# Query features turned by VectorE and through DRAM instead of by TensorE, and gated tiles stored in longer pieces

## The chip, the cores and the metric

The kernel runs on one core of a Trainium2 chip. The metric is the device time of one execution in microseconds (us); the time of a kernel is the median of its runs. The engines are named as in the profile: PE is TensorE's matrix multiply, PEld its weight load, DVE is VectorE, ACT ScalarE, POOL GpSimd, SP SyncE, which issues most of the DMAs. DMAs issued by GpSimd wait in GpSimd's own instruction queue, those of SP in SP's.

## What is computed

A layer over 2048 tokens of width 512, all in float32: the input plus a linear attention with 32 heads and learned softmax features, plus a gated MLP whose gate mixes tokens. Cut to what matters:

```python
def reference(A_x, A_wqkv, A_w_phi, A_wo, B_x, B_w_in, B_w_sp, B_b_sp, B_w_out):
    xn = _layernorm(A_x)
    # A: q, k, v per head of width 16; features = [softmax(p), softmax(-p)], p = q @ w_phi[h]
    #    kv = phi_k^T v, z = sum of phi_k over the tokens
    #    o = (phi_q kv) / (phi_q z + 1e-6);   A = o @ wo
    # B: z = gelu(xn @ w_in); z1, z2 = halves of width 688; z2 = layernorm(z2)
    #    u = z1 * (w_sp @ z2 + b_sp);         B = u @ w_out
    return A_x + A + B
```

## The kernel before

The tokens are 16 tiles of 128. A float32 operand of a large product is split into a rounded part `h` and a rest `l`, and `mm3` makes each product from three matmuls (hence lines 56, 57 and 58).

First part (to about 220 us): the projections of each tile; the query features before their normalisation go to DRAM (`e_d`), and so do the inner halves `z1` (`z1_d`). Second part (to about 290 us): the other halves `z2` and their split. Third part (to about 488 us): the product of `w_sp` with `z2`, pair of tiles by pair of tiles, in seven sub-products per block (`products`, 32 steps `n`), whose left operands are loaded by SP (`wf`) and made by ScalarE and VectorE (`prep_a`) two steps ahead. Behind every fourth step `drain` adds the sub-products up and `gate` multiplies with gelu of `z1`. The gated tiles `u` have the tokens in their partitions and are needed with the features there, for the last product. `turn` does this in two steps: VectorE transposes all 32x32 blocks of the pair (L796), and four DMAs, one for each 32 partitions, store the blocks to `u_d` so that they come to stand in their transposed places (L799). Since a partition then holds runs of only 32 floats that belong together, the pieces have 128 bytes. Pair 6 is stored by GpSimd's queue, all others by SP's. Pair 7 is gated late, in the last part, after pair of tiles 8 (`GATE_LAST`).

Last part (from about 488 us): the loop over pairs of tiles `i`, `i+1`. For each pair TensorE runs

- `project_u(i)`: 15 matmuls of `u` with `w_out`, and two for the last 48 features, into a bank of PSUM (`out`, two buffers),
- `attend`: 32 small matmuls `po` (L952) of the transposed query features `f` with the 64x32 blocks of `kvT`; ScalarE and VectorE split the result into `oT`,
- `project_u(i+1)`, and then `project_o` for both tiles: 12 matmuls each with `wo` on top of the same bank. ScalarE copies the bank to `xr` (L984, three buffers), and GpSimd's queue adds it to the output in DRAM (L985),
- `attend_T(i+2)`: 16 transposes (`ptq`, L935 and L937) of the next pair's query features, which ScalarE copies from PSUM to `f` (L939).

Beside this, `ahead` prepares later tiles: `features(i+3)` normalises the query features of a tile on VectorE (`q_fin`: L543 to L550, from `et` with scratch `qtmp`), and a DMA of GpSimd's queue copies them from the shared slot to their own tile `er` (L906); `load_q` loads `et` for tile `i+5`, and `fetch_u` the gated tile `i+4` (L814, and L815 for the rest), which `split_u` splits into `uh` (ScalarE) and `ul` (VectorE). The slots of `et` and `qtmp` are 16 large buffers (`xz`), shared with other data.

The order of the instructions on each engine comes from a planner that simulates the program with its own costs; where the author wants a certain order, `issue_after` holds an instruction behind another one of its engine. A DMA issued from an engine waits in that engine's queue for what it needs, and everything behind it on that queue waits too.

Of the kernel before, what the change touches and what calls it, by code (L numbers as in the profile page):

```python
# [10 lines left out]
F32 = mybir.dt.float32  # L11
F32R = mybir.dt.float32r
# [21 lines left out]
NP = NT // 2  # L34
# [6 lines left out]
def mixer(ctx: ExitStack, tc: tile.TileContext, x, x_t, wv, wqkT, phi_bd, wo, w_in, wst, b_r, w_out, out):  # L41
    nc = tc.nc
    pe, act, dve, pool, sp = nc.tensor, nc.scalar, nc.vector, nc.gpsimd, nc.sync


    def round_h(eng, h, src):
        if eng is act:
            return act.activation(h, src, AF.Copy).ins  # L48
        return eng.tensor_copy(h, src).ins

    def rest_l(l, src, h, eng=None):
        return (eng or dve).tensor_tensor(l, src, h.bitcast(F32), op=ALU.subtract).ins  # L52
# [22 lines left out]
    dram = ctx.enter_context(tc.tile_pool(name="dram", bufs=1, space=DRAM))  # L75
    e_d = dram.tile([NT, P, NF + 2 * H], F32, name="e_d")
    z1_d = dram.tile([NT, P, FH], F32, name="z1_d")
    u_d = dram.tile([NT, FU, P], F32, name="u_d")
    kvT_d = dram.tile([P, D], F32, name="kvT_d")
    zb_d = dram.tile([P, NF], F32, name="zb_d")  # L80
    nm_d = dram.tile([NT, ND, P], F32, name="nm_d")

    ident = cst.tile([P, P], F32, name="ident")
# [91 lines left out]
    with ExitStack() as p0:  # L175
# [236 lines left out]
        t = xz_tile(2 * D, F32R, "xT").rearrange("p (a b) -> p a b", a=2)  # L412
# [126 lines left out]
    def q_fin(et, tmp, zb):  # L539
# [9 lines left out]
                          den.unsqueeze(2).to_broadcast([P, H, 2]), op=ALU.mult)  # L549
        return e, dve.tensor_tensor(heads(e), heads(e), bc(w, 2 * H), op=ALU.mult).ins  # L550

    QC = 4
    NQ = NT // QC
    NC = NP * NQ
# [150 lines left out]
    for s in range(NT):  # L705
# [4 lines left out]
        n = s // 2  # L710
# [72 lines left out]
    def gate(i, cb, z, u, ut, after=None):  # L783
        cb, first, _ = cb
        with tc.issue_after(after or first):
            act.activation(z[:, :, :FH], z[:, :, :FH], AF.Gelu_apprx_tanh)
        zs = z[:, :, :FH].rearrange("p k (j f) -> p k j f", j=2)
        us = u[:, :, :FH].rearrange("p k (j f) -> p k j f", j=2)
        dve.tensor_tensor(us, zs, cb, op=ALU.mult)
        lo, hi = u[:, :, KF * P:FH], u[:, :, FH:FU].bitcast(F32R)  # L790
        dve.tensor_copy(hi, lo)
        rest_l(lo, lo, hi)

        def turn():
            src = ut.rearrange("p k f -> p (k f)")
            dve.transpose(src, u.rearrange("p k f -> p (k f)"))  # L796
            dst = u_d[2 * i:2 * i + 2].rearrange("k (j a) t -> a (k j) t", a=BL)
            for b in range(0, P, BL):
                (pool if i == NP - 2 else sp).dma_start(dst[:, :, b:b + BL], src[b:b + BL].rearrange("p (m b) -> p m b", b=BL))  # L799

        return turn

    def slot(name, dt=F32):
        return xz_tile(2 * FH, dt, name)
# [6 lines left out]
        return round_h(act, h, t[:rows]), rest_l(l, t[:rows], h)  # L811

    def load_u(i, u, rt):
        sp.dma_start(u, u_d[i, :KF * P].rearrange("(k p) t -> p k t", p=P))  # L814
        sp.dma_start(rt.bitcast(F32), u_d[i, KF * P:])  # L815
        return u, rt

    def split_u(u, rt, h, l):
        lasts[0] = round_h(act, h, u)
        lasts[1] = rest_l(l, u, h)  # L820
        return h, l, rt

    def k_tiles(ap):
        return ap.rearrange("p (k b) -> p k b", b=P)

    def first_gate(i):
        n = KF * P
        a, b = xz_tile(2 * n, F32R, "u_uh"), xz_tile(n + P, F32R, "ul_rt")
        u = load_u(i, k_tiles(a[:, :n]).bitcast(F32), b[:2 * REM, n:n + P])
        return split_u(*u, k_tiles(a[:, n:2 * n]), k_tiles(b[:, :n]))  # L830

    lasts, wu = [None] * 9, []
# [13 lines left out]
            load_w(w_out, rows, h, l, t[c // 2][:, c % 2 * D:(c % 2 + 1) * D])  # L846
            wu.append((h, l))

    g, es, ets = {}, {}, {}
    for n in range(NC):  # L850
        i = SEQ[n][0]
        if n % NQ == 1 and i < NP - 1:
            z = load_z1(i)
        products(n, g)
        if n % NQ == NQ - 1 and i < NP - 1:
            c = gt.tile([P, 2, FU], F32, tag="c", name="c")
            cq = c[:, :, :FH].rearrange("p k (j f) -> p k j f", j=2)
            cb = drain(i, g, cq)
            g = {}
        if n + 3 < NC:  # L860
            raw[n + 3] = load_a(n + 3)
        if n + 2 < NC:
            A[n + 2] = prep_a(n + 2, raw.pop(n + 2))
        if n % NQ == NQ - 1 and i < NP - 1:
            turn = gate(i, cb, z, c, z, prep_a.last)
            if i < NP - 2:
                turn()
        if n == NC - 4:
            stage_w()
        if n == NC - 3:  # L870
            zs = slot("zb", F32R)
            zb, ident_r = zs[:, :NF].bitcast(F32), zs[:, NF:NF + P]
            round_h(act, ident_r, ident)
            sp.dma_start(zb, zb_d)
            uT = [first_gate(0)]
            ets[2] = load_q(2, slot("et"))
            es[2], last = q_fin(ets.pop(2), slot("qtmp")[:, :NF], zb)
        if n == NC - 2:
            es[0], es[1] = first_q(0), first_q(1)
            t = xz_tile((KF + 1) * P, F32R, "u1")  # L880
            us = {1: load_u(1, k_tiles(t[:, :KF * P]).bitcast(F32), t[:2 * REM, KF * P:(KF + 1) * P])}
    cb = drain(NP - 1, g, slot("c").rearrange("p (k j f) -> p k j f", k=2, j=2))
    with tc.issue_after(cb[2]):
        turn()
# [7 lines left out]
    fin = []  # L892

    def fetch_u(i):
        return load_u(i, cw.tile([P, KF, P], F32, tag="u", bufs=4, name="u"),
                      cw.tile([2 * REM, P], F32R, tag="rt", bufs=6, name="rt"))

    def features(s):
        with tc.issue_after(fin[-1]):
            es[s], ins = q_fin(ets.pop(s), slot("qtmp")[:, :NF], zb)  # L900
        fin.append(ins)
        if s == 3:
            return
        e = es[s]
        es[s] = cw.tile([P, NF], F32R, tag="er", bufs=6, name="er")
        lasts[6] = pool.dma_start(es[s].bitcast(F32), e).ins  # L906

    def gated(u):
        return split_u(*u, wk.tile([P, KF, P], F32R, tag="uh", name="uh"), wk.tile([P, KF, P], F32R, tag="ul", name="ul"))

    cw.tile([P, NF], F32R, tag="er", bufs=6, name="er")
# [4 lines left out]
    cw.tile([P, KF, P], F32, tag="u", bufs=4, name="u")  # L916
# [8 lines left out]

    def attend_T(s):

        fs = []
        for g in range(NG):
            pt = pst.tile([P, 2, 2, P], F32, tag="tr", name="ptq")  # L930
            for a in range(2):
                for k in range(2):
                    src = group(es[s + k], 2 * g + a)
                    if src.dtype == F32:
                        pe.transpose(pt[:, a, k], src, ident)  # L935
                    else:
                        pe.transpose(pt[:, a, k].bitcast(F32R), src, ident_r)  # L937
# [141 lines left out]
```

## Time and profile before

| | |
|---|---|
| median of 3 runs | 623.67 us (623.46 to 625.43) |
| profiled execution | 623.2 us, span 621.5 us |
| TensorE busy | 614.0 us, 99% of the span |
| VectorE, ScalarE, GpSimd busy | 507.9, 272.4, 114.0 us |
| granted TensorE clock | 0.999 |
| DMA packets | 90671, of them 47080 under 512 bytes |

The span is the time from the first to the last recorded instruction; the execution takes 1.7 us more. In rows of the timeline stand start and duration in us, engine, line, operation, output and input; in rows of the chain start, duration and what ran; in square brackets stands how long the engine had been idle and who ended the wait. A row such as `DVE ul L52 <- ACT uh L48: 17.0, 6, 10.0` says who waited for whom: total us, times, longest.

### The profile page before, as it was taken

How to read it: one execution, taken by the hardware profiler on the slowest of the kernel's cores; microseconds unless marked ns; L12 is line 12 of the kernel's file. 1: busy time of each engine (PE TensorE's matmuls, PEld its weight loads, DVE VectorE, ACT ScalarE, POOL GpSimd, SP SyncE). 2: the span in 40 equal slices, each digit the busy share in tenths (PEclk: the TensorE clock that was granted, in tenths of full speed). 3: DMA queues.
4: the chain of work that ended last, by engine and by line, in shares of the span. 5: the costliest groups of instructions: out<-in, count | busy, mean ns of one | idle time of the engine just before them, and what ended most of it. 6: DMA issues, size and time to landing. Idle time of an engine off the chain costs nothing.

```text
span 621.5 us, 11434 instructions
## 1 busy us (share of the span) xinstructions
PE 614.0 (99%) x4366; PEld 560.7 (90%) x4366; DVE 507.9 (82%) x903; ACT 272.4 (44%) x436; POOL 114.0 (18%) x198
## 2 busy tenths in 40 slices
PE   8999999999999999999999999999999999999997
PEld 6888888888889999999999999999999887778775
DVE  5999999999977598988979978696969899989211
ACT  5653334323523458885434433343344433334331
POOL 4122333232110025441000000000000212211110
PEclk9999999999999999999999999999999999999999
DMA  8557875665555857002464754637367799984732
GB/s 321 189 137 165 220 188 162 163 162 154 127 163 150 280 210 263 0 1 82 117 139 134 189 100 148 149 100 176 86 196 231 210 311 322 329 244 109 157 41 49
DMA packets 90671, 103.67 MB, mean 167 GB/s; under 512 B 47080, under 2 KB 60136, under 8 KB 90376
## 3 DMA queue, kind: packets, MB, share of 16 engines
q1 hardware_dynamic: 76840, 60.76, 33.9%
q0 software_dynamic: 11472, 36.54, 23.6%
q10 hardware_dynamic: 2304, 5.64, 2.3%
q8 instruction: 34, 0.56, 0.4%
q14 instruction: 21, 0.17, 0.1%
HBM read 61.61 MB, written 30.56 MB: 148 GB/s over the span
## 4 chain that ended last, share of the span: by engine, by line
PE 98%; DVE 1%; ACT 0%; POOL 0%; issue 0%; DVEq 0%; POOLq 0%
PE g L58 11%; PE g L57 11%; PE g L56 11%; PE proj L57 7%; PE proj L56 7%; PE proj L58 7%; PE zps L56 6%; PE zps L58 6%; PE zps L57 6%; PE pout L56 6%; PE pout L58 5%; PE pout L57 5%; PE ptq L937 1%; PE po L952 1%; PE kvps L353 1%; PE pout L966 1%
## 5 line engine op out<-in xcount | busy, mean ns | idle before, releaser
L57 PE MATMUL g<-B,A 128*128 128x344 f32 x448 | 143.3, 320 | 0.0
L56 PE MATMUL g<-B,A 128*128 128x344 f32 x448 | 142.8, 319 | 0.0
L58 PE MATMUL g<-B,A 128*128 128x344 f32 x448 | 140.6, 321 | 0.1
L56 PEld LDWEIGHTS g<-B,A 128*128 128x128 f32 x448 | 84.3, 188 | 0.0
L57 PEld LDWEIGHTS g<-B,A 128*128 128x128 f32 x448 | 84.2, 188 | 0.0
L58 PEld LDWEIGHTS g<-B,A 128*128 128x128 f32 x448 | 83.6, 188 | 0.4 <-DVE A L52 0.4
L48 ACT ACTIVATE A<-S 128x512 fp32r<-128x512 f32 x64 | 39.3, 629 | 76.9 <-DVE S L589 56.2
L56 PE MATMUL proj<-wqk_h,xT 128*128 128x512 f32 x128 | 50.1, 391 | 0.0
L58 PE MATMUL proj<-wqk_h,xT 128*128 128x512 f32 x128 | 49.8, 389 | 0.0
L57 PE MATMUL proj<-wqk_l,xT 128*128 128x512 f32 x128 | 49.8, 389 | 0.0
L121 ACT ACTIVATE e<-e,r_x 128x1024 f32<-128x1024 f32 x26 | 29.8, 1148 | 42.1 <-DVE e L120 41.1
L48 ACT ACTIVATE A<-wf 128x512 fp32r<-128x512 f32 (+1 forms) x64 | 33.1, 519 | 32.7 <-DMA wf<-in_wst 12.7
L52 DVE TENSOR_TENSOR A<-S,A 128x512 fp32r<-128x512 f32 x64 | 42.9, 686 | 5.4 <-ACT A L48 5.1
L56 PE MATMUL zps<-w_0h,xT 128*128 128x344 f32 x128 | 41.1, 321 | 0.0
L56 PE MATMUL zps<-w_1h,xT 128*128 128x344 f32 x128 | 40.9, 319 | 0.0
L58 PE MATMUL zps<-w_0h,xT 128*128 128x344 f32 x128 | 40.8, 319 | 0.0
L58 PE MATMUL zps<-w_1h,xT 128*128 128x344 f32 x128 | 40.6, 319 | 0.0
L57 PE MATMUL zps<-w_1l,xT 128*128 128x344 f32 x128 | 40.6, 317 | 0.0
L57 PE MATMUL zps<-w_0l,xT 128*128 128x344 f32 x128 | 40.6, 317 | 0.0
L754 POOL DMA_DIRECT2D z1t<-z_d x16 | 8.7, 546 | 167.0 <-DMA u_d<-z1t 101.1
L52 DVE TENSOR_TENSOR A<-wf,A 128x512 fp32r<-128x512 f32 (+1 forms) x64 | 35.0, 549 | 1.9 <-ACT A L48 1.8
L124 DVE TENSOR_REDUCE sm<-e 128x64 f32<-128x1024 f32 x26 | 31.1, 1199 | 2.5 <-ACT e L121 2.4
(218 smaller groups left out, 1425.7 us busy)
## 6 DMA issues: line engine op xcount, KB each, us to landing
wf<-in_wst SPq DMA_DIRECT2D x64, 256.0 KB, 3.3
e_d<-e POOLq DMA_DIRECT2D x16, 544.0 KB, 5.0
et<-e_d SPq DMA_DIRECT2D x16, 544.0 KB, 5.8
er<-et POOLq DMA_DIRECT2D x12, 512.0 KB, 5.9
z_d<-z1f ACTq DMA_DIRECT2D x16, 344.0 KB, 3.0
z1t<-z_d POOLq DMA_DIRECT2D x16, 344.0 KB, 5.0
zacc<-e POOLq DMA_DIRECT2D x10, 512.0 KB, 4.9
u<-u_d SPq DMA_DIRECT2D x15, 320.0 KB, 6.1
```

The lines of the kernel that those rows point to most:

```text
L48: return act.activation(h, src, AF.Copy).ins
L52: return (eng or dve).tensor_tensor(l, src, h.bitcast(F32), op=ALU.subtract).ins
L56: pe.matmul(dst, ah, bh, start=start, stop=False)
L57: pe.matmul(dst, ah, bl, start=False, stop=False)
L58: return pe.matmul(dst, al, bh, start=False, stop=stop).ins
L121: softmax_pair.last = less, act.activation(e, e, AF.Exp, scale=scale).ins
L124: dve.tensor_reduce(sm, heads(e), axis=AX.X, op=ALU.add)
L353: i = pe.matmul(kv_acc[k:k + QP, m // 4], vs[:, m * QP:(m + 1) * QP], e[:, m * HP:(m + 1) * HP], start=first and m < 4 and len(ready) == n ...
L754: pool.dma_start(t[:, k, :FH], z1_d[2 * i + k])
L937: pe.transpose(pt[:, a, k].bitcast(F32R), src, ident_r)
L952: lasts[3] = pe.matmul(po[r][c * QP:(c + 1) * QP, k], kvT[rows, m // 2, cols], fs[m // 4][rows, m // 2 % 2], start=True, stop=True).ins
L966: lasts[2] = pe.matmul(p, rt, w, start=False, stop=i == NT - 1 and k == 1).ins
```

## The change

Two parts. For the query features of tiles 10 to 15, `turn_q` takes the place of the copy to `er` and of TensorE's transposes: VectorE transposes the 32x32 blocks of the normalised features into the scratch `qtmp`, and writes the blocks so that those of one 32-token group stand as (m, c, t): m counts groups of 32 features in a stretch of 128, c the eight stretches. Then 256 floats in a row belong to one row of `q_d`, four DMAs store them in pieces of 1024 bytes, and a fifth DMA loads the tile back whole, all by GpSimd's queue. `attend_T` then only returns views of the loaded tile: the 256 columns that `po` reads are eight runs of 32, for two tiles of four 32-token groups. The tiles `er` become pairs, with three buffers in place of six, and share them with the new tiles.

For the gated tiles the same order of blocks is used, so that 160 floats (640 bytes) of a partition belong together; the last 96 columns of each tile go apart, to `ur_d`, still in pieces of 128 bytes. `turn` now has three transposes and eight DMAs. `load_u` loads a tile as it lies, 2560 bytes for each partition, and `split_u` puts the blocks in order while it reads.

```diff
-    u_d = dram.tile([NT, FU, P], F32, name="u_d")
+    u_d = dram.tile([NT, P, KF * P], F32, name="u_d")
+    ur_d = dram.tile([NT, 2 * REM, P], F32, name="ur_d")
+    q_d = dram.tile([NT, P, NF], F32, name="q_d")
...
+    TQ = 10
+    def turn_q(s, dst, e, f, eng):
+        NC8 = NF // P
+        dve.transpose(dst.rearrange("p (m c t) -> p m c t", c=NC8, t=BL), e.rearrange("p (c m j) -> p m c j", c=NC8, j=BL))
+        w = NC8 * BL
+        for b in range(P // BL):
+            eng.dma_start(q_d[s, :, b * w:(b + 1) * w].rearrange("(m j) w -> j m w", j=BL),
+                          dst[b * BL:(b + 1) * BL].rearrange("p (m w) -> p m w", w=w))
+        eng.dma_start(f[:, s % 2], q_d[s])
...
         def turn():
             src = ut.rearrange("p k f -> p (k f)")
-            dve.transpose(src, u.rearrange("p k f -> p (k f)"))
-            dst = u_d[2 * i:2 * i + 2].rearrange("k (j a) t -> a (k j) t", a=BL)
+            m, r = src[:, :2 * KF * P], src[:, 2 * KF * P:]
+            for k in range(2):
+                dve.transpose(m[:, k * KF * P:(k + 1) * KF * P].rearrange("p (m c t) -> p m c t", c=KF, t=BL),
+                              u[:, k, :KF * P].rearrange("p (c m j) -> p m c j", c=KF, j=BL))
+            dve.transpose(r.rearrange("p (k f) -> p k f", k=2), u[:, :, KF * P:])
+            eng = pool if i == NP - 2 else sp
             for b in range(0, P, BL):
-                (pool if i == NP - 2 else sp).dma_start(dst[:, :, b:b + BL], src[b:b + BL].rearrange("p (m b) -> p m b", b=BL))
+                w = b // BL * KF * BL
+                eng.dma_start(u_d[2 * i:2 * i + 2, :, w:w + KF * BL].rearrange("k (m j) w -> j (k m) w", j=BL),
+                              m[b:b + BL].rearrange("p (m w) -> p m w", w=KF * BL))
+                eng.dma_start(ur_d[2 * i:2 * i + 2, :, b:b + BL].rearrange("k (a j) t -> j (k a) t", j=BL),
+                              r[b:b + BL].rearrange("p (a t) -> p a t", t=BL))
...
     def load_u(i, u, rt):
-        sp.dma_start(u, u_d[i, :KF * P].rearrange("(k p) t -> p k t", p=P))
-        sp.dma_start(rt.bitcast(F32), u_d[i, KF * P:])
+        sp.dma_start(u, u_d[i])
+        sp.dma_start(rt.bitcast(F32), ur_d[i])
...
     def split_u(u, rt, h, l):
-        lasts[0] = round_h(act, h, u)
-        lasts[1] = rest_l(l, u, h)
+        u, hb, lb = u.rearrange("p (b c t) -> p c b t", c=KF, t=BL), *(y.rearrange("p c (b t) -> p c b t", t=BL) for y in (h, l))
+        lasts[0] = round_h(act, hb, u)
+        lasts[1] = rest_l(lb, u, hb)
...
+    def er_pair(name):
+        return cw.tile([P, 2, NF], F32R, tag="er", bufs=3, name=name)
...
     def features(s):
         with tc.issue_after(fin[-1]):
-            es[s], ins = q_fin(ets.pop(s), slot("qtmp")[:, :NF], zb)
+            tmp = slot("qtmp")[:, :NF]
+            es[s], ins = q_fin(ets.pop(s), tmp, zb)
         fin.append(ins)
         if s == 3:
             return
+        if s >= TQ:
+            if s % 2 == 0:
+                ft[s] = er_pair("f").bitcast(F32)
+            turn_q(s, tmp, es.pop(s), ft[s - s % 2], pool)
+            return
         e = es[s]
-        es[s] = cw.tile([P, NF], F32R, tag="er", bufs=6, name="er")
+        if s % 2 == 0:
+            ep[s] = er_pair("er")
+        es[s] = ep[s - s % 2][:, s % 2]
         lasts[6] = pool.dma_start(es[s].bitcast(F32), e).ins
...
     def attend_T(s):
 
+        if s in ft:
+            t = ft[s].rearrange("p k (b c t) -> p (k b) c t", c=NF // P, t=BL)
+            return [t[:, :, 2 * g:2 * g + 2].rearrange("p b c t -> p c b t") for g in range(NG)]
         fs = []
```

More of the change, by code (lines that the diff above doesn't have):

```diff
@@ L828, in first_gate @@
         a, b = xz_tile(2 * n, F32R, "u_uh"), xz_tile(n + P, F32R, "ul_rt")
-        u = load_u(i, k_tiles(a[:, :n]).bitcast(F32), b[:2 * REM, n:n + P])
+        u = load_u(i, a[:, :n].bitcast(F32), b[:2 * REM, n:n + P])
         return split_u(*u, k_tiles(a[:, n:2 * n]), k_tiles(b[:, :n]))
@@ L847, in stage_w @@
             wu.append((h, l))
-    g, es, ets = {}, {}, {}
+    g, es, ets, ft, ep = {}, {}, {}, {}, {}
     for n in range(NC):
@@ L880, in mixer @@
             t = xz_tile((KF + 1) * P, F32R, "u1")
-            us = {1: load_u(1, k_tiles(t[:, :KF * P]).bitcast(F32), t[:2 * REM, KF * P:(KF + 1) * P])}
+            us = {1: load_u(1, t[:, :KF * P].bitcast(F32), t[:2 * REM, KF * P:(KF + 1) * P])}
     cb = drain(NP - 1, g, slot("c").rearrange("p (k j f) -> p k j f", k=2, j=2))
@@ L894, in fetch_u @@
     def fetch_u(i):
-        return load_u(i, cw.tile([P, KF, P], F32, tag="u", bufs=4, name="u"),
+        return load_u(i, cw.tile([P, KF * P], F32, tag="u", bufs=4, name="u"),
                       cw.tile([2 * REM, P], F32R, tag="rt", bufs=6, name="rt"))
+    def er_pair(name):
+        return cw.tile([P, 2, NF], F32R, tag="er", bufs=3, name=name)
     def features(s):
         with tc.issue_after(fin[-1]):
-            es[s], ins = q_fin(ets.pop(s), slot("qtmp")[:, :NF], zb)
+            tmp = slot("qtmp")[:, :NF]
+            es[s], ins = q_fin(ets.pop(s), tmp, zb)
         fin.append(ins)
@@ L909, in gated @@
         return split_u(*u, wk.tile([P, KF, P], F32R, tag="uh", name="uh"), wk.tile([P, KF, P], F32R, tag="ul", name="ul"))
-    cw.tile([P, NF], F32R, tag="er", bufs=6, name="er")
+    er_pair("er")
     wo_h = cw.tile([P, ND, D], F32R, name="woh")
@@ L915, in mixer @@
     kvT = cw.tile([P, 2 * NG, HP], F32, name="kvT")
-    cw.tile([P, KF, P], F32, tag="u", bufs=4, name="u")
+    cw.tile([P, KF * P], F32, tag="u", bufs=4, name="u")
     wo_l = cw.tile([P, ND, D], F32R, name="wol")
```

## The prediction

> **What bounds the kernel now.** I read the summary page first, then what TensorE waited for, then the chain of waits in order of time through the last part, and last the timelines of VectorE, GpSimd, ScalarE and SP around the code that changes. Page and waits:
>
> ```profile
> span 621.5 us, 11434 instructions
> PE 614.0 (99%) x4366; PEld 560.7 (90%) x4366; DVE 507.9 (82%) x903; ACT 272.4 (44%) x436; POOL 114.0 (18%) x198
> PE 98%; DVE 1%; ACT 0%; POOL 0%; issue 0%; DVEq 0%; POOLq 0%
> ...
> PE idle L382 <- POOL ident masks.py:199: 1.8, 1, 1.8
> PE ptq L937 <- DVE c L772: 0.4, 1, 0.4
> PE proj L56 <- ACT wv_h L48: 0.2, 1, 0.2
> PE proj L57 <- DVE wv_l L52: 0.2, 1, 0.2
> ```
>
> TensorE is busy 614.0 of 621.5 us, its own work is 98% of the chain that ended last, and its four waits come to 2.6 us. So time is won where TensorE's own work gets shorter and lost where something makes it wait; work saved on the other engines or the DMA engines pays nothing by itself.
>
> The edit takes work from TensorE in one place: the transposes `ptq` for tiles 10 to 15, three of eight pairs. The chain (start, duration, piece) around those groups, with the attention matmuls `po` that use the result:
>
> ```profile
> 568.76 0.23 PE pout L58
> 568.99 1.34 PE ptq L937 x16
> 570.33 0.30 PE pout L56
> 570.63 0.23 PE pout L57
> ...
> 574.30 1.02 PE po L952 x32
> ...
> 584.91 1.31 PE ptq L937 x16
> 586.21 0.30 PE pout L56
> ...
> 600.81 1.34 PE ptq L937 x16
> 602.14 0.30 PE pout L56
> ...
> 606.11 1.02 PE po L952 x32
> ```
>
> `pout` matmuls follow each other at 0.23 us; the first one behind the transposes takes 0.30. A pair's transposes hold the chain 1.31 to 1.34 us plus 0.07.
>
> **The change part by part.**
>
> *Off TensorE: three pairs of transposes.* 1.34 + 1.31 + 1.34 + 3 x 0.07 = 4.2 us, all on the path that sets the end. Twelve ScalarE copies `ptq` to `f` go too; ScalarE is busy 44%, they count nothing. `project_u` now follows `project_o` at once, and needs the PSUM bank of `out` that ScalarE's `xr` copy of two tiles earlier empties:
>
> ```profile
> 583.35 0.60 ACT L984 ACTIVATE xr<-pout 128x512 f32<-128x512 f32 x1 [3.85 <-PE pout L58]
> ```
>
> It ends at 583.95, and without the transposes the bank is wanted at 584.91: 0.96 us to spare. Taken as 0; with that cover gone TensorE would wait out the difference.
>
> *On VectorE: six transposes of 128x1024.* The rows are VectorE around tiles 14 and 15 (`et` L550 is the last step of a tile's features), GpSimd's copy of the finished features, and the median landing of such DMAs in two stretches:
>
> ```profile
> 568.52 1.22 DVE L543 TENSOR_TENSOR qtmp<-et,zb 128x1024 f32<-128x1024 f32 x1
> 569.65 1.71 DVE L796 STREAM_TRANSPOSE zt<-z1t 128x1472 f32<-128x1472 f32 x1
> ...
> 575.15 1.22 DVE L550 TENSOR_TENSOR et<-et 128x1024 f32<-128x1024 f32 x1
> 579.53 0.83 DVE L52 TENSOR_TENSOR ul<-u,uh 128x640 fp32r<-128x640 f32 x1 [1.96 <-ACT uh L48]
> ...
> 590.31 0.83 DVE L52 TENSOR_TENSOR ul<-u,uh 128x640 fp32r<-128x640 f32 x1 [9.96 <-ACT uh L48]
> ...
> 595.43 0.83 DVE L52 TENSOR_TENSOR ul<-u,uh 128x640 fp32r<-128x640 f32 x1 [2.20 <-ACT uh L48]
> ...
> 569.22 0.54 POOL L906 DMA_DIRECT2D er<-et  x1
> ...
> 576.92 0.54 POOL L906 DMA_DIRECT2D er<-et  x1 [6.06 <-DVE et L550]
> ...
> er<-et POOLq DMA_DIRECT2D x2, 512.0 KB, 5.3
> ...
> out<-xr POOLq DMA_DIRECT2D x3, 256.0 KB, 6.2
> ```
>
> 1.71 x 1024/1472 = 1.2 us each, so by tile 15 VectorE is at most 6 x 1.2 = 7.2 us later. In return nothing is shorter there, but it sat idle 9.96 us before 590.31, so what comes after finds its old place. The price on the path is whether the last tile is ready. Tile 15's features end at 576.37; turned at the latest at 583.6. Then GpSimd issues four writes of 0.54 (the last starts 1.6 later), they land 5.3 after, the read of `q_d` is issued and lands 6.2 after: 583.6 + 13.1 = 596.7. `po` of pair 14 wants it at 606.11 - 4.2 = 601.9. Spare 5.2 us: 0 on the path. Tile 13 comes two of GpSimd's steps earlier (2 x 7.7 us) and 2.4 us less delayed, and is wanted one new pair earlier, (606.11 - 574.30)/2 - 1.4 = 14.5: no tighter.
>
> *The added wait.* GpSimd's `out` for tile 8, ScalarE's copy for tile 11, and SP's last load of `et`:
>
> ```profile
> 568.34 0.87 POOL L985 DMA_DIRECT2D out<-xr  x1 [6.49 <-ACT xr L984]
> ...
> 584.99 0.60 ACT L984 ACTIVATE xr<-pout 128x512 f32<-128x512 f32 x1 [1.04 <-PE pout L58]
> ...
> 550.38 0.55 SPq L536 DMA_DIRECT2D et<-e_d  x1
> ```
>
> GpSimd's queue stands at the read of `q_d` until the four writes have landed, 1.6 + 5.3 + 0.54 = 7.4 us per tile; tiles come 7.7 us apart (569.22 to 576.92), 1.2 more with the transpose. Queued behind are the next tile's writes and the additions to `out`. `xr` has three buffers, so ScalarE's copy for tile 11 needs the landing of `out` of tile 8, issued 16.6 us before it: 7.4 of delay and 6.2 of landing still fit. Taken as 0. Scratch `qtmp` is held until its writes land, `et` is given back earlier; SP loads the last `et` 18 us before its use at 568.52.
>
> *`po` reads its features in another order.* 256 moving columns were one run of 256, now eight runs of 32 elements (128 bytes) 1024 bytes apart. No row shows TensorE reading its moving operand in pieces. Bounds: 0 (as many elements; and not below, since the same number of columns passes the array) and twice the 1.02 us, 3 x 1.02 = 3.1 us. I take 0, the nearest row being `po` itself. The Trainium skill, "SBUF — State Buffer", section "Door 1: The DMA port swizzle", says that an SRAM line has 16 bytes and that reads lose only when too few of them hit each line; by it runs of 128 bytes cost nothing and the sum stays at 4.2, and no run here shows it yet.
>
> *Gated tiles in 640-byte pieces.* VectorE's one transpose of 1472 columns becomes three with the same columns, for each of eight pairs; a start costs under 0.19 (L546's whole instruction), so up to 0.4 us more a pair. The store becomes eight issues: 4 x 256 pieces of 640 bytes and 4 x 192 of 128, for 4 x 1472 of 128. Seven of the pairs do this beside the token mixing (290 to 488 us):
>
> ```profile
> 572.75 0.19 DVE L546 SCALAR_TENSOR_TENSOR et<-et 128x32 f32<-128x32 f32 x1
> ...
> 290.00:314.00 24.00, 23.88 (x152) 23.60 (x151) 20.94 (x45) 10.55 (x18) 1.19 (x2) 1.00 0.40 116
> 362.00:386.00 24.00, 24.00 (x154) 24.00 (x153) 17.32 (x36) 9.75 (x17) 1.06 (x2) 1.00 0.57 138
> ...
> DVE S L588 <- DMA wf<-in_wst: 19.1, 4, 4.9
> ...
> 364.87 3.79 SPq L799 DMA_DIRECT2D u_d<-z1t  x4
> ...
> 512.15 0.37 SPq L814 DMA_DIRECT2D u<-u_d  x1
> ```
>
> (Columns of the windows: span, then busy time of TensorE, its weight loads, VectorE, ScalarE, GpSimd.) TensorE loses 0.12 us of 24 in the first stretch and nothing in the second, where VectorE idles 6.7, so 0.4 is covered. On SP eight issues take 8 x 0.37 = 3.0 us by the load of `u`, or 8 x 0.95 = 7.6 by the old store, against 3.79. Behind them stand the `wf` loads of the next steps. VectorE waits up to 4.9 us for these already without TensorE noticing, as operands are made two steps ahead: 0 by the lower row, and with fewer pieces I take the lower; if the cover went, up to 3.8 us a pair. Pair 7, turned at 571.36, is wanted at 602.14 - 4.2, 26 us later; pair 6 goes by GpSimd at the head of the last part, two pairs before GpSimd's turned tiles. Loads of `u` have 128 pieces of 2560 bytes instead of 640 of 512; the splits `uh` and `ul` read in runs of 32, at worst at twice the 0.83 us of `ul`, on engines with idle time before them. All 0.
>
> **Sum.** The profiled execution took 623.2 us (621.5 span, 1.7 around it). 623.2 - 4.2 = 619.0, span 617.3. The median shown, 623.67, stands 0.47 above the profiled run, so 619.5 for the median.
>
> **The rivals.**
>
> *The last tiles come late* (chance 0.09). The spread of landings of `out`, and the window in which tile 15's read would run (the last two columns are the share of the DMA engines that is busy, and GB/s):
>
> ```profile
> DMA to landing us min/median/max: 3.8/6.2/10.0
> ...
> 585.00:601.00 16.00, 16.00 (x110) 12.73 (x109) 2.94 (x4) 5.83 (x11) 1.84 (x3) 1.00 0.36 76
> ```
>
> VectorE's order is a planner's; if landings take as long as the worst `out` (10.0) in both steps, 583.6 + 1.6 + 10 + 10 = 605.2, 3.3 us late: 622.8; a typical case costs half, about 621.2. For it: a path of 13 us in place of one on TensorE and ScalarE; against: 5.2 us spare, and DMA engines that are busy 0.36 of the time by then.
>
> The Trainium skill, "VectorE: DVE Perf Modes", section "Rules for kernel authors", sends a 128x128 transpose to TensorE where the result may land in PSUM, as it does here; by that rule the detour is the dearer way and this rival the likely one. The trace speaks against it here: TensorE is what is short, and the detour ends before it is wanted.
>
> *`po` pays for its pieces* (0.05): at twice its time 619.5 + 3.1 = 622.6.
>
> *TensorE waits elsewhere for what it saves* (0.04): the bank of `out` comes over 0.96 us later, because ScalarE's `xr` waits for a buffer whose `out` stands behind a read in GpSimd's queue. Three pairs at 1.4 us: no change, 623.7.
>
> *Slower* (0.05): the transposes, late in program order, are placed on VectorE behind the `ul` of the same tile. For tile 15 that `ul` ends at 596.26, less 2.8 for two shortened pairs; 593.5 + 1.2 + 13.1 = 607.8, and `po` waits 5.9 us. Tile 13 behind the `ul` at 579.53 is late by as much (580.4 - 1.4 + 1.2 + 13.1 = 593.3 for 601.9 - 14.5 = 587.4). With both, 619.5 + 11.8 = 631.3. A transpose of tile 15 costs from an end after 588.8, and outweighs the whole gain from 593.0. Against: 9.96 us of idle VectorE where it fits.
>
> **How the numbers follow.** The forecast, 619.5, has 0.77, its own range 618.6 to 620.6. With the late tiles at 621.2 and `po` up to its bound of 622.6 the range is 618.6 to 622.6, which leaves out the slow case and the no-gain case. The low end is 619.5 less the 0.4 us wait of `ptq` on the drain, which the order could remove, and 0.5 for the distance of a run from its median. A measurement of this kernel tells some 0.3% (1.9 us) from no change. Faster: 0.77 and half of the late tiles, 0.82; within 0.3%: the rest of those, `po` and the no-gain case, 0.13; slower 0.05.
>
> **What would show it.** The page's line on packets:
>
> ```profile
> DMA packets 90671, 103.67 MB, mean 167 GB/s; under 512 B 47080, under 2 KB 60136, under 8 KB 90376
> ```
>
> Right: tiles 8 and 9 are the last with a `ptq`, pairs from 10 on about 1.4 us shorter, TensorE's waits still under 3 us, `po` of the three pairs at 1.02, six transposes of 1.2 us, DMA packets under 512 B down from 47080 to about 6100 (8 x 4 x 192). Wrong: a TensorE wait on `q_d` or on `xr`, `po` over 1.02, or idle TensorE between 290 and 488.

## The result and the profile after

The changed kernel took 618.75 us (median of six runs, 618.28 to 619.21) beside 623.69 us for the kernel before (median of six): a ratio of 0.9914, 95% interval 0.9901 to 0.9927. The forecast was 619.5, its range 618.6 to 622.6. It is faster, as forecast, and the median lies 0.75 us under the forecast; by the ratio, 0.9914 x 623.67 = 618.3, the result is 0.3 us below the low end of the range. The ratio is here that of the two means, 618.75 to 624.11, and not of the medians. Two more sets of runs of the same kernel, on other chips, gave 619.83 and 619.70 (experiments e9 and e16), with ratios of 0.9934 [0.9916, 0.9952] and 0.9918 [0.9890, 0.9946]. One execution of e6 below, 626.99 us at a granted clock of 0.993, counts as slow and is left out of e6's ratio.

The profiled execution took 618.89 us. Its page:

```profile
span 617.0 us, 11407 instructions
PE 610.3 (99%) x4318; PEld 557.1 (90%) x4318; DVE 517.6 (84%) x925; ACT 269.6 (44%) x424; POOL 128.8 (21%) x226
...
DMA packets 55534, 106.81 MB, mean 173 GB/s; under 512 B 12136, under 2 KB 22248, under 8 KB 55240
...
PE idle L384 <- POOL ident masks.py:199: 1.8, 1, 1.8
PE proj L57 <- DVE wv_l L52: 0.2, 1, 0.2
```

TensorE has 48 instructions fewer (three pairs of 16 transposes) and waits 2.0 us in all. The chain of waits through the last part, the rows with `ptq` and `po` and its last row:

```profile
553.09 1.31 PE ptq L974 x16
...
558.38 1.02 PE po L989 x32
...
572.86 1.02 PE po L989 x32
...
587.33 1.02 PE po L989 x32
...
601.80 1.02 PE po L989 x32
...
612.59 0.42 DVE xr L1026
```

The `ptq` at 553.09 stands where it stood, to the hundredth. After it the three `po` come 1.44, 2.87 and 4.31 us earlier than 574.30, 590.20 and 606.11, still at 1.02 us each: 1.43 to 1.44 for each pair, all of it and nothing else. VectorE's last operation starts 4.31 us earlier than in the kernel before, where it was

```profile
616.90 0.42 DVE L989 TENSOR_TENSOR xr<-pend,xr 128x256 f32<-128x256 f32 x1 [0.77 <-PE pend L58]
```

and the tail behind it to the end of the span is 0.19 shorter (3.99 for 4.18). 4.31 + 0.19 = 4.5, the 621.5 - 617.0 of the spans.

A good measure for what follows is the stretch from the start of the first `po` (494.36 in the timelines of both kernels) to the start of VectorE's last operation: 122.54 us before and 118.23 after. It leaves out what differs between executions ahead of the last part, and the tail.

So the path did what the forecast said. Two things remained: what the other half of the change, the long pieces, adds (the forecast put it at 0), and why the result came in lower.

### The profile page after: what moved, and what is told of

The parts are those of the page before. It is cut to its first block, busy times and chain, and to the rows that moved or that the text cites. A ratio compares the mean times of both kernels' runs of the same rounds, so it can differ in the third digit from the quotient of the medians.

```text
span 617.0 us, 11407 instructions
## 1 busy us (share of the span) xinstructions
PE 610.3 (99%) x4318; PEld 557.1 (90%) x4318; DVE 517.6 (84%) x925; ACT 269.6 (44%) x424; POOL 128.8 (21%) x226
## 4 chain that ended last, share of the span: by engine, by line
PE 95%; DMA 3%; DVE 0%; SPq 0%; ACT 0%; issue 0%; DVEq 0%; ACTq 0%
PE g L58 11%; PE g L57 11%; PE g L56 11%; PE proj L57 7%; PE proj L56 7%; PE proj L58 7%; PE zps L56 6%; PE zps L57 6%; PE zps L58 6%; PE pout L56 6%; PE pout L58 5%; PE pout L57 5%; PE po L989 1%; PE kvps L355 1%; PE pout L1003 1%; DMA wst__2228<-in_w_in 1%
```

## Experiments

Each kernel ran beside the kernel before on the same chip; that kernel's medians in the five groups of runs were 623.89 (e1 to e4), 623.65 (e5 to e8), 623.86 (e9 to e12), 624.27 (e13 to e16) and 624.37 (e17, e18).

### The two halves, each alone

**e1: the long pieces, no tile turned by VectorE.**

```diff
-    TQ = 10
+    TQ = NT
```

> The gated tiles in 640-byte pieces, the query features turned by TensorE as before (the tiles er as pairs). Theory A, only TensorE's removed transposes count: as the kernel before, ratio 0.9995 to 1.0005, some 623.7 us, 16 transposes ptq in each of eight pairs. Theory B, the short pieces themselves cost time in most executions of the kernel before, which its profiled one (623.2 us, under all six timed runs) did not show: 0.5 to 1 us faster, ratio 0.9985 to 0.9992, and a narrower spread than the 2 us of before.

Measured: 626.60 (seven runs, 625.76 to 627.52), ratio 1.0041 [1.0026, 1.0056]: slower than the kernel before, which neither side had expected. The chain is that of before, and VectorE's last operation starts at 616.97, for 616.90. What is longer lies behind it, in GpSimd's last instruction (rows by line and kind: count, shortest/median/longest in ns, first and last start), first of before, then of e1:

```profile
L1075 POOLq DRAIN  x3: 40/93/5107, 615.6 to 621.2; - x3
```

```profile
L1112 POOLq DRAIN  x3: 45/93/8214, 615.7 to 624.4; - x3
```

The longest of the three takes 8.2 us in place of 5.1. Without these 3.1 us the time would be 623.5, that of before.

**e2: the turned query tiles, gated tiles stored and loaded as before.**

```diff
-    u_d = dram.tile([NT, P, KF * P], F32, name="u_d")
+    u_d = dram.tile([NT, FU, P], F32, name="u_d")
...
-        sp.dma_start(u, u_d[i])
+        sp.dma_start(u, u_d[i, :KF * P].rearrange("(k p) t -> p k t", p=P))
```

(and `turn` and `split_u` as before)

> Tiles 10 to 15 turned by VectorE and through DRAM, the gated tiles in 128-byte pieces as before. Theory A: all of the gain, ratio 0.9914 to 0.9925, 618.7 to 619.2 us, three pairs 1.43 us shorter each. Theory B: 0.5 to 1 us less gain than the whole change, 619.3 to 619.7 us, and the wide spread of before.

Measured: 622.57 (twelve runs, 619.64 to 624.70), ratio 0.9971 [0.9953, 0.9989]. Neither theory had this. Turning alone keeps 1.3 us of the 4.2 in the median, and its times spread over 5 us. Since long pieces alone give nothing, the two halves are worth more together than their sum: without its 640-byte pieces the changed kernel would lose 0.0037 to 0.0057 of the time, 2.3 to 3.6 us (by the ratios, as the sets ran on different chips). The profiled execution was the fastest of the twelve, and not a typical one: its first `po` starts at 492.67, where all other profiles have 493.81 to 495.36. The time was gained between 220 and 280 us, where its trace counts 392 matmuls and the others 378 to 383; why is not known. From the first `po` to the last operation it took 119.41 us, 1.2 more than the changed kernel. In it the chain ran over pair 7's gated tile, on SP and ScalarE:

```profile
570.89 8.02 SPq L812 DMA_DIRECT2D u_d<-zt  x4
...
583.35 0.38 SPq L827 DMA_DIRECT2D u<-u_d  x1
...
590.35 0.74 ACT L48 ACTIVATE uh<-u 128x640 fp32r<-128x640 f32 x1 [7.38 <-DMA u<-u_d]
590.99 1.07 ACT L48 ACTIVATE oT<-po 128x512 fp32r<-128x512 f32 x2
```

ScalarE stood 7.38 us at the split of tile 14, and behind that split, in its own queue, stands `oT` of pair 12, which TensorE needs next; here TensorE waited 0.4 us for it. In the kernel before and in the changed one the same split waits for TensorE only, not for the load:

```profile
589.54 0.74 ACT L48 ACTIVATE uh<-u 128x640 fp32r<-128x640 f32 x1 [1.99 <-PE pout L57]
```

```profile
586.67 0.74 ACT L48 ACTIVATE uh<-u 128x640 fp32r<-128x640 f32 x1 [2.53 <-PE pout L57]
```

In the changed kernel SP issued this load at 582.27, 1.1 us earlier than in e2, and it was there by 586.67, at most 4.4 us later, where the load in e2 took 6.9.

**e3: the kernel before, once more.** No edit.

> The kernel before, unchanged, against itself. Both theories: ratio 1.000 within 0.001; median 623.5 to 624.0. Under A the profile of this execution shows where an ordinary run is longer than the 621.5 us span of the profile before: in DMA waits at the start or the end. Under B it shows TensorE waiting beside the stores of gated tiles, 300 to 490 us.

Measured: 623.69 (twelve runs, 623.02 to 627.92), ratio 1.0003 [0.9983, 1.0022]. Two sets of the same kernel can't be told apart within about 0.2% either way; the kernel before has single executions of up to 4 us more.

### Which gated tiles need the long pieces

**e5 and e6: turned query tiles, with long pieces for pair 7 only (e5) and for pairs 0 to 6 only (e6).**

```diff
+    def wide(i):
+        return i == NP - 1      # e6: i < NP - 1
...
+            if not wide(i):
+                dve.transpose(src, u.rearrange("p k f -> p (k f)"))
+                dst = uo_d[2 * i:2 * i + 2].rearrange("k (j a) t -> a (k j) t", a=BL)
...
```

> Tiles 10 to 15 turned as in the change; of the gated tiles only pair 7 is stored and loaded in the long pieces, pairs 0 to 6 in 128-byte pieces. Theory P7: the turn alone lost its gain because pair 7's store and load came late, and its split on ScalarE stands ahead of the oT of pair 12 in that engine's queue (in the profile of the turn alone uh of tile 14 waited 7.4 us for its load). Then this has nearly the whole gain: 618.5 to 619.5 us, in a narrow spread, uh of tile 14 no longer waiting for a DMA. Rival L, the crowded loads at 488 to 521 us (640 pieces of 512 bytes a tile) make ScalarE and VectorE late: as the turn alone, 621 to 623 us, widely spread.

> The other half: pairs 0 to 6 in long pieces, pair 7 in 128-byte pieces, tiles 10 to 15 turned. P7: as the turn alone, 621 to 623 us, spread over 3 us or more, uh of tile 14 waiting for its load in the profile. L: 618.5 to 619.5 us.

Measured: e5 620.69 (twelve runs, 619.78 to 624.71), ratio 0.9948 [0.9926, 0.9971]; e6 619.63 (twelve runs, 617.47 to 626.99; without the longest the median is 619.50 and the highest 620.23), ratio 0.9922 [0.9905, 0.9938]. Each takes most of the loss away. Of the 1.2 us between the two, 0.9 is the tail (the longest DRAIN of GpSimd is 6.05 us in e5, 5.15 in e6, 6.19 in e2), so ahead of the tail they are about even; e6 lies within the sets of the changed kernel (618.75 to 619.83), so no median shows what pair 7's pieces add to it. In both profiles the stretch from the first `po` is 118.23 us, as in the changed kernel. So the medians can't settle how the loss is shared. That it arises at two places, pair 7 near the end and the loads in the stretch where the last part begins, is read from the profiles of e13 to e15 below. The split of tile 14, first of e5, then of e6:

```profile
586.91 0.74 ACT L48 ACTIVATE uh<-u 128x640 fp32r<-128x640 f32 x1 [2.52 <-PE pout L57]
```

```profile
589.13 0.74 ACT L48 ACTIVATE uh<-u 128x640 fp32r<-128x640 f32 x1 [5.06 <-DMA u<-uo_d]
```

In e5 it waits for TensorE again; in e6 it still waits 5.06 us for its load, though TensorE does not feel it in that execution.

### Where turning alone loses its gain

**e13, e14, e15: the kernel of e2 again, for the profiles of other executions.**

> Turning alone once more, for the profile of another execution (the profiled one was the fastest, 619.64, with its last VectorE operation at 612.08 and a tail of 5.4 us behind it). Theory L: where the execution takes 621 to 624 us, the last VectorE operation is late by as much (613.5 to 616.5) and TensorE waits 1.5 to 4 us for uh, oT or f; the tail stays under 6.5. Rival D: the last operation stays within 0.5 of 612.1 and the tail is 7 to 10 us.

> The same again: L puts the difference between executions ahead of the last VectorE operation, as waits of TensorE; D puts it behind.

> The same again: L puts the difference between executions ahead of the last VectorE operation, as waits of TensorE; D puts it behind.

They took 624.00, 624.24 and 627.43 us. The last VectorE operation starts at 616.51, 616.68 and 619.99, for 612.08 in e2's profile; from the first `po` that is 122.08, 122.57 and 124.63 us, 3.9, 4.3 and 6.4 more than in the changed kernel. The longest DRAIN stays at 6.06 to 6.11 us (6.19 in e2): the difference between executions lies ahead of the last operation, as theory L said. (Against the changed kernel, with 4.90 to 5.30 in its three profiles, the tail of turning alone is 0.8 to 1.3 us longer in all four: that much of its loss is tail, and the rest, some 2 us in the median by subtraction, is put down to waits.) The chain of e13 over the stretch around 500 us and again at the end:

```profile
494.59 8.94 DMA u<-u_d
503.63 0.75 ACT uh L48
504.40 0.83 DVE ul L52
505.39 1.22 DVE et L551
...
580.28 7.32 DMA u_d<-zt
587.74 6.96 DMA u<-u_d
594.81 0.74 ACT uh L48
595.54 0.49 ACT oT L48
```

A load of a gated tile takes 8.94 us, ScalarE and VectorE do their split when it comes, and only then, in VectorE's order, come the query features (`et`) that TensorE waits to transpose. TensorE waited 1.1 and 0.4 us there. At the end it is pair 7, stored (7.32) and loaded (6.96) one after the other, and TensorE waited 1.6 us for `oT`. In e14 the only added wait is one of 2.55 us for `et` at 507.77, behind a load of a gated tile of 8.86 us. In e15 a load of `et` took 10.49 us and VectorE's `oT` came behind it:

```profile
520.59 0.80 PE L58 MATMUL pout<-woh,oT 128*128 128x512 f32 x1 [2.86 <-DVE oT L52]
```

What this wait did to TensorE's clock is in the windows (span, TensorE busy and matmuls, granted clock, DMA share, GB/s):

```profile
516.00:518.00 2.00, 1.73 (x8) 1.00 1.07 365
518.00:520.00 2.00, 0.00 (x0) 0.97 1.06 366
520.00:522.00 2.00, 1.41 (x3) 0.50 0.61 228
522.00:524.00 2.00, 2.00 (x6) 0.50 0.07 27
524.00:526.00 2.00, 2.00 (x6) 0.50 0.81 239
526.00:528.00 2.00, 2.00 (x9) 0.82 1.01 349
```

The granted clock fell to 0.50 for some 6 us. From the `po` ahead of the wait to the next one it took 21.92 us (511.61 to 533.53), in the changed kernel 15.90 (510.63 to 526.53, e16): 6.0 us for a wait of 2.9.

The delay at the start begins ahead of the gated tile: SP issues 16 loads of `wof` (pieces of `wo`) before it, and they held SP's queue for 10.0, 10.5 and 10.4 us in e13 to e15, for 8.0 in e2 and 8.4 in the changed kernel. The delay alone is not the loss. It is also in the profiles of e1, e4, e11, e17 and e18 (9.5 to 10.2 us), all with long pieces, and there TensorE has no added wait between 490 and 540 us; in e3, with short pieces and no turned tile (9.9 us), it waits 0.4. So the long pieces do not remove this delay, they leave room for it; and that e5's profile, with 7.8 us, has no wait at the start says nothing about the short pieces there. Why the loads of `wof` hold the queue longer in some executions is open.

### The tail

**e8: the kernel before with four small DMAs more on GpSimd's queue.**

```diff
+    pad_d = dram.tile([4, P, 8], F32, name="pad_d")
...
+    for k in range(4):
+        pool.dma_start(pad_d[k], ident[:, 8 * k:8 * k + 8])
```

> The kernel before with four small DMAs more on GpSimd's queue (4 KB each, to a scratch tensor that nothing reads), as many DMAs on that queue as the pieces alone have. If the number of GpSimd's DMAs decides how long its drain at the end takes (5.1 us before, 8.2 us with the pieces alone): drain 8 us, 626.5 us. If the kind or place of those DMAs decides: drain 5 us, 623.7 us.

Measured: 623.93 (ten runs), ratio 1.0002 [0.9982, 1.0022], longest DRAIN 5.23 us. The number of GpSimd's DMAs does not set it.

**e10: long pieces alone, and none stored by GpSimd.**

```diff
-            eng = pool if i == NP - 2 else sp
+            eng = sp
```

(beside `TQ = NT`)

> Pieces alone (no query tile is turned by VectorE), and pair 6's pieces issued by SP like all others, so that GpSimd stores no gated tile. Theory L: without GpSimd's eight stores its last instruction is as short as before (about 5 us, not 8.2), and what is left of the pieces shows: 622.0 to 623.2, with a spread under 1.5 us. Rival D (the long tail of pieces alone has nothing to do with the stores on GpSimd): 626 to 627 again, with 8 us in the last instruction of GpSimd. If pair 6 is wanted too early for SP, the chain shows a wait on u_d near 505 us.

Measured: 632.37 (six runs, 631.49 to 635.34), ratio 1.0138 [1.0117, 1.0160]; the longest DRAIN is 7.75 us. So the long tail comes with long pieces without turning, whoever stores them; L's expectation failed, and the theory has no account of the tail. The other 6 us are pair 6's store: SP issues it at 491.4 to 495.3, ahead of its loads of `wof` and `et`. ScalarE's `oT` comes late behind the split of `wof`, `et` lands only at 504.4, and TensorE waits 2.0, 1.0 and 0.5 us, with the clock at 0.50 after the first. The DRAIN over all kernels is 4.9 to 5.3 us in before, after, e3, e6 to e9, e11 and e16 to e18, 5.4 and 5.6 in e4 and e12, 6.1 to 6.2 for turning alone and in e5, 7.8 to 8.2 for long pieces alone. About the first 5 us of it run beside SP's own end: SP reaches its first DRAIN of the end at 620.6 us before and at 620.5 in e1, and the spans end at 621.5 and 624.7. What GpSimd's DRAIN takes beyond that is what lengthens the time. Why it differs between the programs is open.

### How much room the detour has

**e7: tile 15 makes a second trip, DRAM to DRAM, before it is read.**

```diff
+        last = q_d
+        if s == NT - 1:
+            eng.dma_start(q2_d[s], q_d[s])
+            last = q2_d
-        eng.dma_start(f[:, s % 2], q_d[s])
+        eng.dma_start(f[:, s % 2], last[s])
```

> The changed kernel with one more trip for tile 15 alone: its turned features are copied from DRAM to DRAM before they are loaded, some 6.5 us more on that path. In the changed kernel's trace the load is issued at 593.81, lands 5.4 us later and is wanted at 601.80: 2.6 us to spare. If that reading holds, TensorE waits 3.5 to 4.5 us at po of pair 14 and the kernel takes 622.2 to 623.2 us. If the detour is hidden with more room than the rows show: 618.7 us.

Measured: 618.92 (four runs, 618.44 to 619.36), ratio 0.9909 [0.9873, 0.9944]: no wait. GpSimd's queue in e7:

```profile
591.73 0.55 POOL L567 DMA_DIRECT2D q_d<-q_d  x1 [3.64 <-DMA q_d<-qtmp]
595.67 0.56 POOL L569 DMA_DIRECT2D f<-q_d  x1 [3.40 <-DMA q_d<-q_d]
```

The extra trip took 3.9 us (591.73 to 595.67), but the stores before it had left 0.8 earlier and landed sooner than in the changed kernel, so the read was issued only 1.86 later than there (593.81) and landed in time for `po` at 601.77. What failed in the expectation was the 6.5 us for the trip; 2.6 us to spare are not refuted, as 1.86 fit into them.

**e4: tiles 8 to 15 turned.** `TQ = 8`. One more pair off TensorE.

> Four pairs turned instead of three (tiles 8 to 15). If a removed group of 16 transposes is worth 1.43 us on the chain and the detour stays hidden: 1.43 us under the changed kernel, 617.3 us, ratio to before 0.9897. If GpSimd's queue, which holds 8 to 9 us for each tile, or VectorE, which has 0.5 us idle of 16 between 505 and 553 us, is full there: a TensorE wait at po of pair 8 or 14 of 1 to 3 us, 618.5 to 620.5 us.

Measured: 620.13 (nine runs, 618.54 to 624.26), ratio 0.9945 [0.9923, 0.9968]. The fourth pair brings nothing: TensorE waits at pair 8,

```profile
PE po L989 <- DMA f<-q_d: 2.0, 1, 2.0
```

because GpSimd's queue stood at the read of tile 8 until 542.93 and stored tile 9, which VectorE had turned by 540.92, only from 543.76 on.

**e11 and e12: tiles 8 to 15 (e11) or 6 to 15 (e12) turned and read back by SP's queue.**

```diff
-        eng.dma_start(f[:, s % 2], q_d[s])
+        sp.dma_start(f[:, s % 2], q_d[s])
```

> Tiles 8 to 15 turned, as in the run from tile 8 on, but the turned tile is read back by SP's queue, so that GpSimd's queue doesn't stand at the read and tile 9's stores leave at once (540.9 where they left at 543.8). If the queue held by the read cost the 2.0 us of pair 8: TensorE no longer waits at pair 8, 618.75 - 1.4 = 617.3 (617.0 to 618.0). Rival: DVE is what is late for tile 9, or SP's loads behind the read are: a wait of 1.5 us or more stays, 618.7 to 620.5.

> As the run before, from tile 6 on: one more pair off TensorE, 1.4 us less to do, but two more transposes and eight more stores in the crowded stretch around 505 to 540 us. If there is room: 615.9. If VectorE, whose stretch before 540 us is nearly full, is late by the two transposes (2.4 us) there: 617.5 to 619.5, with a wait of PE on f or oT at pair 6 or 8. I think the second likelier.

Measured: e11 619.12 (six runs, 618.40 to 621.11), ratio 0.9923 [0.9903, 0.9942]; e12 622.68 (twelve runs, 619.54 to 624.93), ratio 0.9978 [0.9960, 0.9995]. The wait at pair 8 is gone in e11 (`po` at 557.22), and so far the queue was the cause. But at pair 12 there is a new one, since the read of tile 13 stands on SP's queue behind the loads of pair 7's tiles:

```profile
581.12 0.43 SPq L837 DMA_DIRECT2D rt<-ur_d  x1
581.71 10.86 SPq L564 DMA_DIRECT2D f<-q_d  x3
...
588.43 1.10 PE L989 MATMUL po<-f,kvT 64*32 64x256 f32 x32 [2.27 <-issue]
```

The profile names no releaser for this wait; I put it down to the read, since the same wait in e12, 3.6 us, is one for `f<-q_d`. In e12 the granted clock is 0.54 and 0.61 in the two windows of 2 us from 590 us on. Its median lies above both expectations. VectorE, which I had held for the likelier bound, was not late.

**e17 and e18: tiles 8 to 15 turned, the early reads by SP and the late ones by GpSimd.**

```diff
-        eng.dma_start(f[:, s % 2], q_d[s])
+        (sp if s < 10 else eng).dma_start(f[:, s % 2], q_d[s])      # e18: s < 12
```

> Tiles 8 to 15 turned; tiles 8 and 9 are read back by SP's queue, 10 to 15 by GpSimd's. If the waits of the two runs from tile 8 on came from the queues alone: TensorE waits for no f, last VectorE operation at 611.2, median 1.4 us below the changed kernel's 619.3: 617.9 (617.3 to 618.5). Rival: the extra pair's stores and loads make something else late: 619 to 620.

> The same with tiles 8 to 11 read back by SP's queue, 12 to 15 by GpSimd's. The queues alone: 617.9 as well, no wait at pair 8, 10 or 12. Rival: SP's reads of tiles 10 and 11 delay pair 7's store (569 us) or loads of u: 619 to 620.

Measured: e17 618.14 (four runs, 617.83 to 618.43), e18 617.87 (four runs, 617.43 to 618.85), ratios 0.9896 [0.9879, 0.9914] and 0.9896 [0.9880, 0.9911]. TensorE's waits in e18, and its chain:

```profile
PE idle L384 <- POOL ident masks.py:199: 1.8, 1, 1.8
PE pz L631 <- DVE zhl L52: 0.3, 1, 0.3
...
537.47 1.34 PE ptq L974 x16
542.77 1.02 PE po L989 x32
557.25 1.02 PE po L989 x32
571.72 1.02 PE po L989 x32
```

No wait for a turned tile is left, and from 542.77 the pairs follow each other in 14.47 us. From the first `po` to the last operation e17 took 116.96 us and e18 116.80, for 118.23 in the changed kernel: the fourth pair pays its 1.4 us. (e17's last operation starts at 611.99, not at the expected 611.2, since its first `po` came at 495.03.) These are the fastest kernels of this case: beside the three sets of the changed kernel (all 18 runs: median 619.3) e18 is 1.5 us faster, an estimate across chips.

### The result's own scatter

**e9 and e16: the changed kernel again, on two other chips.** No edit.

> The changed kernel itself, unchanged, beside the kernel before. Theory L (long pieces keep the loads of the last part early, so executions stop being lengthened): the median lies within 0.6 us of the fastest execution, between 618.3 and 619.2, against about 623.7 for before, whose fastest is 622.0 to 622.6. Rival N (the six runs so far were lucky): the median is 619.3 to 620.5 with a spread like that of turning alone (619.6 to 624.7).

> The changed kernel a third time. If its sets scatter by chance around one value, as the first two (618.75 and 619.83) suggest: 619.2, between 618.6 and 620.0. If chips differ: near one of the two, with before shifted in the same way, so that the ratio is between 0.991 and 0.994 all the same.

Measured: e9 619.83 (six runs, 619.26 to 621.21), e16 619.70 (six runs, 619.17 to 620.30). The profiled executions took 619.36 and 619.31, and the stretch from the first `po` is again 118.23 and 118.24 us. The median of e9 lies in the range of rival N, its spread of 2.0 us well under the 5 us of turning alone: the first six runs were low by luck, and the narrower spread holds. With the first set the eighteen runs have a median of 619.3 and the set medians lie 1.1 us apart, less than a ratio's interval is wide (0.9901 to 0.9927 is 1.6 us).

## Why the prediction was right or wrong

*Off TensorE, 4.2 us: right, a little small.* The three pairs gave 1.44, 1.43 and 1.44 us, for 1.41, 1.38 and 1.41 by the `ptq` groups and 0.07 each; the tail gave 0.19 more, which was no part of the sum.

*Bank of `out`, 0.96 us to spare: held.* No wait of TensorE on ScalarE's `xr` in any run with turned tiles and long pieces.

*VectorE's six transposes, 1.2 us each: right* (1.24), and so was the end of the last one, "at the latest at 583.6":

```profile
581.20 1.25 DVE L559 STREAM_TRANSPOSE qtmp<-et 128x1024 f32<-128x1024 f32 x1
...
583.39 0.56 POOL L564 DMA_DIRECT2D f<-q_d  x1 [4.87 <-DMA q_d<-qtmp]
583.94 0.94 POOL L1022 DMA_DIRECT2D out<-xr  x1
585.68 2.24 POOL L562 DMA_DIRECT2D q_d<-qtmp  x4 [0.80 <-issue]
587.91 0.97 POOL L1022 DMA_DIRECT2D out<-xr  x1
593.81 0.57 POOL L564 DMA_DIRECT2D f<-q_d  x1 [4.93 <-DMA q_d<-qtmp]
```

*Spare of 5.2 us for tile 15: too large by half.* Turned at 582.45, its stores left only at 585.68, behind the read of tile 14 and an `out` on GpSimd's queue. The read at 593.81, with the median landing of 5.4 us, is there at 599.2 for `po` at 601.80: 2.6 us. I had worked out that the queue is held 7.4 us for each tile (measured for tile 14: 576.29 to 583.95, 7.7) and not put that into the path of the next tile. It cost nothing here; at pair 8 the same omission would have cost the whole gain of a further pair (e4).

*`po` in pieces of 32, 0 with a bound of 3.1 us: right at 0.* 1.02 us before and after. By the Trainium skill, "SBUF — State Buffer", section "Door 1: The DMA port swizzle", runs of 128 bytes fill whole lines of 16 bytes and lose nothing; the trace agrees.

*Gated tiles in long pieces, "all 0": wrong, and the step of the mechanism that failed.* As a price on the path it stands: pieces alone leave VectorE's last operation at 616.97 for 616.90 (their tail of 3.1 us more was not foreseen, and is not there with turned tiles). But the forecast's 4.2 us rested on these pieces. Without them turning gives 1.3 us in the median (e2). That the sum still came near the result was luck in this point: what turning loses without the pieces, 2.3 to 3.6 us, and what the pieces give back were both left out, and cancel. About 1 us of the loss is the longer tail; for the rest the chains of e13 and e15 show the two places where it arises. Behind the step stood the sentence "Pair 7, turned at 571.36, is wanted at 602.14 - 4.2, 26 us later". That looked at TensorE's use of the tile. ScalarE wants it before: `uh` of tile 14 stands in ScalarE's queue ahead of `oT` of pair 12, at 589.54 in the trace of before. There the load was issued at 583.11 and lands, by the median of 6.1, at 589.2: 0.3 us to spare, and by then two pairs have made TensorE 2.87 us earlier:

```profile
571.39 5.95 SPq L799 DMA_DIRECT2D u_d<-zt  x4
583.11 0.38 SPq L814 DMA_DIRECT2D u<-u_d  x1
```

The store was to be seen, and the row of `uh` too. The other place, the loads around 500 us, is where the long pieces lower the DMA share of 505 to 521 us, from 1.05 before to 0.89 after (a sign and no proof: e5 has 1.04 there and no wait in its profile):

```profile
505.00:521.00 16.00, 16.00 (x107) 12.87 (x106) 15.52 (x25) 5.83 (x10) 2.46 (x4) 1.00 1.05 328
```

```profile
505.00:521.00 16.00, 16.00 (x107) 12.86 (x106) 15.52 (x25) 5.83 (x10) 2.32 (x4) 1.00 0.89 288
```

*Packets under 512 bytes, "about 6100": wrong.* There are 12136. Pair 7 alone removes 47464 - 42408 = 5056 of the 5120 counted for it (e2 and e5), pairs 0 to 6 remove 47464 - 17192 = 30272 of 35840 (e6): some 5600 pieces of these pairs are still recorded under 512 bytes. Why was not followed.

*Profiled 619.0, median 0.47 above it: the term of the sum that was off, and with it the low end.* The profiled time was right: 618.89, with 4.5 us off the span for 4.2. Profiled executions took 618.89, 619.36 and 619.31; the medians stand 0.14 below, 0.47 and 0.39 above them. So 0.61 of the 0.75 us by which the median came in under the forecast lie in this term. The first set of six happened to be the lowest, 0.6 under the 619.3 of all eighteen, which the forecast of 619.5 meets. The low end, 618.6, allowed 0.5 for a single run's distance from its median, and nothing for that of a set: medians of six lay 1.1 us apart. Nor did it allow for the other side of the ratio. Two of the six executions of the kernel before took 624.74 and 625.43 us, so that its mean stands 0.42 over its median; by the medians the ratio would be 0.9921, 618.7 us. These two things put the ratio's 618.3 out of the range.

*The rivals.* No tile came late, `po` paid nothing, and VectorE placed each transpose at once. "TensorE waits elsewhere for what it saves" (no change, 623.7) names what turning alone does, though at ScalarE's `uh` and VectorE's `et` and `oT` rather than at the bank of `out`. The prices of tiles later than some 2.5 us were too low, since they counted the wait alone: behind waits of 2.5 to 3.6 us the clock halved as well.

## What to carry to other kernels

A load is wanted when the first instruction that stands behind it in an engine's queue is wanted, not when its own data reach TensorE: follow the queue, not the data. When the bounding engine gets shorter, look in the old trace for rows whose idle time ends on TensorE and whose load lands just before: here such a load, with 0.3 us to spare, was one of two places that took away some 2 of 4.2 us. Where the next tile follows at once, a read that waits for its own store should not share a queue with that tile's store; splitting reads over two queues gave a further pair its full 1.4 us.

## What the hardware showed that I had not expected

The clock behind a wait. After waits of TensorE of 2.5 (e14), 2.9 (e15) and 3.6 us (e12) the granted clock fell to 0.50 to 0.61 for some 3 to 6 us; after 2.0 (e4) and 2.3 us (e11) it stayed at 1.00, while in e10 one of 2.0 us, followed by a stretch at 0.50, did the same as the long ones. The Trainium skill, "TensorE: Matmul & The Clock Gate", section "Part 1: The HAM clock gate (the "warmup" mystery)", says that the clock halves after an idle window of about 3.4 us that runs freely. The traces agree on the halving, and shorter waits sufficed here: the limit that these runs show lies near 2 to 2.5 us, and differs between executions.

GpSimd's last DRAIN, 4.9 to 8.2 us at the end of every profiled execution, follows the program and not the number of its DMAs; what it takes beyond about 5 us lengthens the time.

A stream transpose of 128x1024 float32 costs 1.24 us on VectorE, as much as an elementwise pass over the same data (1.22), and a trip of 512 KB from DRAM to DRAM took 3.9 us from its issue to that of the read behind it.
